# A hand-written order with two copies on another engine, some tasks in other places and one buffer in another slot

## The chip, the cores and the metric

The kernel runs on one core of a Trainium2 chip. The metric is the time of one execution on the device in microseconds (us), as the median of several runs. The kernel before takes 345.94 us in the median of three runs (345.81 to 346.79).

The engines of the core are TensorE (PE in the profile, PEld for its weight loads), VectorE (DVE), ScalarE (ACT), GpSimd (POOL) and SyncE (SP). SP and POOL do little but issue transfers (DMA) here. Every engine works through its own list of instructions in order; where one needs another's result, or a buffer that another still uses, it waits, and all that stands behind it in its list waits too.

## The reference

Two independent layers for a sequence of 2048 steps and 1024 channels; their outputs stand side by side.

```python
def _A_ref(q, k, v, shift_k, ssm_k, ssm_D):
    for t in range(ks):                      # ks = 4
        k_shift = k_shift + k_pad[:, t:t + S, :] * shift_k[:, ks - 1 - t][None, None, :]
    kv = k_shift * v
...
    y_f = kv_f * kf_f[None, :, :, :]         # Fourier transforms of kv and of ssm_k, length 2 S
    y = irfft2(y_f)[:, 0, :S, :]
    y = y + kv * ssm_D[None, None, :]
    return q * y

def _B_ref(x, Lambda_re, Lambda_im, B_re, B_im, C_re, C_im, log_dt, Dskip):
...
    Bu = jnp.einsum("bld,pd->blp", x + 0j, B_bar)
    for t in range(L):
        h = Lam_bar[None, :] * h + Bu[:, t, :]
        hs.append(h)
    y = 2.0 * jnp.einsum("blp,dp->bld", hseq, Cmat).real + x * Dskip[None, None, :]
    return y
...
return jnp.concatenate([a, b], axis=-1)
```

Layer A is a long convolution, done by Fourier transforms; layer B is a linear recurrence with complex coefficients.

## The kernel before

The whole program is one list of some 1,500 words, `ORDER`. A word names a task, its arguments and the buffers that it takes, such as `sh.20:p5p6`: task sh for group 20, in the PSUM banks 5 and 6. A loop at the end of `full_kernel` goes through the words and calls the task's function, so the words' order is the order of the instructions on every engine, and the letters behind the colon say which buffer is used: `p` one of 8 PSUM banks, `a` a place in an arena of 53 units in SBUF, `h` one of three state buffers, `w` one of three tables. A task whose buffer is still in use waits. Nothing else decides the schedule.

Layer B goes through 16 chunks i of 128 steps. `U.i.jp.jl` forms the inputs of the recurrence on PE (16 products of 128x128, line L464), `ue.i.jp` copies them from PSUM (L473). On DVE follow `r1.i` and `r2.i` (a rotation: product and sum, L487 and L498), two scans `sc.i` (L504), and `r3.i` and `r4.i`, which rotate back (L487 and L510). `yq.i.k` (L538) or `y.i.dh.part` (L520, L523) form the output on PE, `ye.i.dh` copies it from PSUM (L556), `ysp.i` writes it out from SP's queue (L564), `ysg` and `ysh` write halves (L560). `x.i` loads a chunk of the input, transposing it (L447). Ahead of the loop stand the tables of the rotation (`tabA1`, `tabA2`, `par_rest`) and the transposed weights: `bT.j.w` transposes on PE (L415), `bc.j.w` on ACT (L431) or `bcv.j.w` on DVE (L427, L429) copies.

Layer A does the transform in two stages with matrix products. The first (`am`, `ae`) goes through memory; the second works on 32 groups g, two to an index i = g // 2. `lh.i` and `lk.i` load the two operands (L677), `lw.i` the table (L672). `sh.g` and `sk.g` are products of 64x64 with the table (four each, L688), `she.g.l` (L697) and `ske.g.l` (L704) copy them from PSUM. `sw.i.q` (from POOL) and `swp.i.q` (from SP) copy one half of a buffer with its real and imaginary rows swapped (L708). `pr.i` multiplies the two spectra on DVE (L714). `sa.g` transforms back on PE (eight products, L726), `sae.g.dh` copies (L734), `vst.i` writes to memory (L737), `vl.n` loads back (L742), `a3.n.dh` is the last stage on PE (two products, L754), `a3e.n.dh` copies (L761), `qp.r` loads q (L747), `qm.r` multiplies with q on DVE (L763), and `osp` and `ost` write out.

A copy from PSUM is a task in two variants, made by one helper:

```python
def either(nm, f):
    E[nm] = lambda *a: f(nc.scalar.copy, *a)
    E[nm + "v"] = lambda *a: f(nc.vector.tensor_copy, *a)
```

So `ye.10.1` runs on ACT and `yev.10.1` on DVE.

Of the kernel before, what the change touches and what calls it, by code (L numbers as in the profile page):

```python
# [156 lines left out]
r3.11:a17 sh.30:p4p0 sh.31:p2p6 U.12.3.1:p3 she.20.0 she.31.0:a9 sw.10.1 U.12.3.0 lk.10:a45 U.12.0.0:p5 she.30.1
she.31.1 lk.12:a39 she.30.0 ue.12.3 lk.15:a43 swp.10.0 swp.15.0 U.12.0.1 sa.22:p4p3 r4.11 sae.22.0:a37 sa.23:p1p2
U.12.2.0:p6 sae.23.1 sw.15.1 U.12.2.1 uev.12.2 ue.12.0 sae.23.0 sk.20:p0p5 sae.22.1 ske.20.0:a28 sk.21:p7p2 skev.21.0
yq.11.0:p4p1 sk.30:p6p0 ske.20.1 ske.30.1:a18 yq.11.1 sk.31:p3p0 yq.11.2 lw.12:w1 vst.7 lk.14:a47 ske.30.0 ske.31.0  # L160
sh.25:p3p7 yq.11.3 skev.21.1 sh.24:p5p2 ske.31.1 pr.10 she.25.0:a24 sa.20:p0p3 she.25.1 sa.21:p7p6 she.24.1 yq.11.4
she.24.0 vst.11 pr.15 vst.9 sae.20.1:a29 sae.20.0 yq.11.5 r1.12:a2 sk.24:p3p2 sae.21.1 sa.31:p5p0 ysp.10 sae.31.1:a20
saev.31.0 lw.14:w0 yq.11.6 sa.30:p6p0 ske.24.0:a22 sae.30.0 skev.24.1 yq.11.7 saev.21.0 sk.25:p6p5 swp.12.0 sh.28:p7p2
sae.30.1 U.13.3.0:p0 yev.11.1:a28 ye.11.0 sk.29:p1p3 ske.25.1 cy.12:h1 shev.28.1:a16 ske.25.0 sk.28:p2p5 sh.29:p6p4
she.28.0 she.29.0 U.13.3.1 U.13.1.1:p7 r2.12 x.15:a0 ske.28.0:a5 ske.29.0 U.13.1.0 ske.28.1 U.13.2.1:p6 ue.13.3:a10
swp.12.1 lh.13:a13 sc.12.1 lw.13:w2 lk.13:a45 she.29.1 sh.26:p0p4 qp.0:a48 sw.14.1 ske.29.1 she.26.0:a41 sh.27:p5p3
she.27.0 U.13.2.0 pr.12 U.13.0.0:p2 she.27.1 she.26.1 ue.13.2 U.13.0.1 ue.13.1 sk.26:p3p1 swp.14.0 ske.26.0:a1
sk.27:p6p4 sa.25:p7p0 U.15.3.0:p5 ue.13.0 ske.27.1 sae.25.1:a38 sc.12.0 r3.12:a12 U.15.0.1:p2 U.15.3.1 pr.14 U.14.2.1:p3
U.15.0.0 sae.25.0 swp.13.1 ske.27.0 vst.15 ske.26.1 uev.15.3:a50 sw.13.0 sa.29:p7p6 sa.28:p0p1 ue.15.0 sa.24:p4p2 vst.6
ysp.11 sae.29.1:a34 U.15.1.0:p5 sae.24.0 r4.12 sae.24.1 qp.5:a6 vst.10 saev.29.0 sae.28.0 U.15.1.1 U.14.2.0 pr.13  # L170
sa.27:p6p4 ue.15.1 cy.13:h2 sae.28.1 sae.27.0:a8 yq.12.0:p0p7 r1.13:a12 sa.26:p1p2 yq.12.1 yq.12.2 saev.26.0 qp.6:a20
sae.27.1 yq.12.3 U.14.3.1:p5 U.14.1.0:p1 vst.12 sae.26.1 ue.14.2:a24 U.14.0.1:p3 U.14.3.0 vst.14 U.14.1.1 qp.1:a18
U.15.2.0:p4 vst.13 U.14.0.0 ue.14.3 yq.12.4 yq.12.5 ue.14.1 r2.13 sc.13.0 sc.13.1 vl.3:a38 r3.13:a12 r4.13 yq.13.0:p2p1
yq.13.1 yq.13.2 ue.14.0 yq.13.3 r1.14:a40 r2.14:h0 cy.14 vl.13:a44 yq.12.6 vl.1:a16 vl.9:a32 yq.12.7 a3.13.1:p5 sc.14.1
sc.14.0 r3.14:a24 a3e.13.1:a4 vl.2:a2 ye.12.0:a41 U.15.2.1 a3.13.0:p3 a3.1.0:p5 yq.13.4 vl.12:a46 yq.13.5 uev.15.2
# [667 lines left out]
```

## Time and profile before

| | |
|---|---|
| median of three runs | 345.94 us (345.81 to 346.79) |
| the profiled execution | 345.12 us |
| its span, first instruction to last | 343.4 us |
| PE busy | 331.0 us, 96% |
| DVE busy | 326.1 us, 95% |
| ACT busy | 273.0 us, 80% |
| POOL busy | 66.8 us, 19% |
| transfers of SP's queue, share of 16 DMA engines | 66.6% |
| transfers of POOL's queue, share of 16 DMA engines | 25.6% |

The span is the part of an execution in which the program's instructions run; the rest of the time lies around it. A row of the timeline has the start in us, the duration in us, the engine, the line, the operation, what it writes and reads, and how many neighbouring instructions of one form it merges; in brackets stands how long the engine sat idle before it, and what released it. A row of SP (SPq) is the issue of a transfer, not the transfer. Rows of PE merge groups of four or more products. A row of the busy time by stage gives for each engine the busy time and the number of instructions.

### The profile page before, as it was taken

Reading aid. Unit: us, or ns where it says so; the run is one execution under the profiler, and the core shown is the slowest. Engines: PE = TensorE matmul, PEld = TensorE weight load, DVE = VectorE, ACT = ScalarE, POOL = GpSimd, SP = SyncE. Lnnn points to the kernel's source line nnn. Section 1 sums busy time; section 2 is a strip of 40 time slices with the busy share of each in tenths; the row PEclk is TensorE's granted clock in tenths of the full one; section 3 lists DMA queues with packets and bytes.
Section 4 is the critical chain, followed back from the end, with each engine's and each line's share of the span. In section 5 each row is a group of like instructions: output and inputs, shape, how many; then the busy total and the mean of one; then the engine's idle time right before and its main releaser. Section 6 shows DMA issues by size and latency. Waiting matters only on the chain. (4 is left out here: it accounts for less than half of the span.)

```text
span 343.4 us, 11818 instructions
## 1 busy us (share of the span) xinstructions
PE 331.0 (96%) x5105; PEld 231.4 (67%) x5105; DVE 326.1 (95%) x262; ACT 273.0 (80%) x523; POOL 66.8 (19%) x108
## 2 busy tenths in 40 slices
...
GB/s 191 366 283 304 282 264 296 253 300 351 234 303 255 326 268 266 247 296 249 297 321 271 324 348 264 351 254 272 318 320 290 296 326 315 208 370 296 353 371 245
DMA packets 62944, 100.83 MB, mean 294 GB/s; under 512 B 29422, under 2 KB 31742, under 8 KB 62892
## 3 DMA queue, kind: packets, MB, share of 16 engines
q1 hardware_dynamic: 53452, 67.65, 66.6%
q0 software_dynamic: 9440, 32.42, 25.6%
q8 instruction: 40, 0.66, 0.8%
...
## 5 line engine op out<-in xcount | busy, mean ns | idle before, releaser
L464 PEld LDWEIGHTS <-BT 128*128 128x128 bf16 x2048 | 117.0, 98 | 13.8 <-issue 9.2
L464 PE MATMUL bank<-arena,BT 128*128 128x128 bf16 x2048 | 124.6, 220 | 0.3 <-ACT BT L431 0.3
L538 PE MATMUL bank<-CT,gslot 64*64 64x512 bf16 x1408 | 88.0, 378 | 0.0
L504 DVE TENSOR_TENSOR_SCAN gslot<-rtab,gslot 128x1040 bf16<-128x1040 f32 x32 | 72.9, 2310 | 0.8
L538 PEld LDWEIGHTS <-gslot 64*64 64x64 bf16 x1408 | 38.4, 107 | 30.2 <-issue 1.3
L473 ACT CAST arena<-bank 128x512 bf16<-128x512 f32 x61 | 37.1, 641 | 11.4 <-PE bank L464 10.5
L614 ACT CAST arena<-bank 128x512 bf16<-128x512 f32 x64 | 36.2, 646 | 7.8 <-PE bank L608 7.2
L520 PE MATMUL bank<-CT,gslot 128*128 128x512 bf16 x160 | 39.4, 379 | 0.1
L487 DVE TENSOR_TENSOR arena<-gslot,Z 128x4096 bf16<-128x4096 bf16 x16 | 36.6, 2288 | 0.5
L704 ACT CAST arena<-bank 128x512 bf16<-128x512 f32 x60 | 33.6, 612 | 4.3 <-PE bank L688 3.1
L714 DVE TENSOR_TENSOR arena<-arena 128x4096 bf16<-128x4096 bf16 x16 | 36.4, 2282 | 0.2
L487 DVE TENSOR_TENSOR arena<-arena,Z 128x4096 bf16<-128x4096 bf16 x16 | 36.5, 2282 | 0.0
L697 ACT CAST arena<-bank 128x512 bf16<-128x512 f32 x62 | 33.5, 618 | 3.7 <-PE bank L688 2.3
L734 ACT CAST arena<-bank 128x512 bf16<-128x512 f32 x60 | 32.9, 609 | 4.4 <-PE bank L726 4.3
L665 ACT CAST arena<-bank 128x512 bf16<-128x512 f32 x64 | 34.3, 631 | 1.9 <-PE bank L657 1.8
L588 DVE TENSOR_TENSOR arena<-arena 128x4096 bf16<-128x4096 bf16 (+3 forms) x16 | 29.9, 1881 | 0.0
L668 POOL DMA_DIRECT2D Ys_h<-arena x32 | 23.5, 737 | 28.5 <-ACT arena L665 26.0
L617 POOL DMA_DIRECT2D Ys_kv<-arena x16 | 11.1, 710 | 87.5 <-ACT arena L614 86.0
L761 ACT CAST arena<-bank 128x512 bf16<-128x512 f32 x26 | 13.7, 599 | 15.3 <-PE bank L754 15.1
L556 ACT CAST arena<-bank 128x512 bf16<-128x512 f32 x30 | 17.8, 602 | 9.7 <-PE bank L538 4.9
L520 PEld LDWEIGHTS <-gslot 128*128 128x128 bf16 x160 | 14.3, 98 | 16.5 <-issue 1.3
L688 PE MATMUL bank<-arena,wslot 64*64 64x512 bf16 x256 | 22.4, 382 | 0.8 <-DMA wslot<-a_c_W 0.8
...
## 6 DMA issues: line engine op xcount, KB each, us to landing
...
Ys_h<-arena POOLq DMA_DIRECT2D x32, 256.0 KB, 4.7
...
arena<-arena SPq DMA_DIRECT2D x17, 256.0 KB, 4.0
...
```

Source lines behind the costliest of these rows:

```text
L464: nc.tensor.matmul(pu[:, w, jl, :], BT[:, 2 * jp + jl, w, d, :], xT[:, d, :], start=(d == 0), stop=(d == ND - 1))
L473: cp(st["u", i][:, :, 2 * jp:2 * jp + 2, :], st.pop(("pu", i, jp)))
L487: nc.vector.tensor_mul(m, s_, win(Z))
L504: nc.vector.tensor_tensor_scan(gf, rtab[:].rearrange("p j t -> p (j t)"), gf, 0.0, ALU.mult, ALU.add)
L520: nc.tensor.matmul(py, h[:, w, j, 2:GW], CT[:, j, w, dh * 512:(dh + 1) * 512], start=(j == 0 and w == 0), stop=False)
L538: mm = nc.tensor.matmul(st["py", i, dh][cols, cs(r)], lhs(dh, rows, c), rhs(dh, rows), start=first, stop=last)
L614: cp(st["ysb", n2][:, p, dh * 512:(dh + 1) * 512], st.pop(("pa", n2, p, dh)))
L665: cp(o, st.pop(("pb", hf, s, e, r)).rearrange("p (n c t) -> p n c t", n=2, c=2))
L697: cp(st["hab", i][:, 0, a, l, :], st.pop(("ps", "h", g, l)))
L704: cp(st["x16", i][:, a, l, :], st.pop(("ps", "k", g, l)))
L714: nc.vector.tensor_mul(hab, st.pop(("x16", i)).rearrange("p a l d -> p (a l d)").unsqueeze(1).to_broadcast([P, 2, 2 * D]), hab)
L734: cp(st["vsb", i][:, a, dh * 512:(dh + 1) * 512], st.pop(("pv", g, dh)))
```

## The change

Only the list changes; the same tasks run with the same arguments. Three words change in themselves, and twelve words stand in other places:

- `yev.10.1` becomes `ye.10.1` and `uev.15.2` becomes `ue.15.2`: two copies from PSUM go from DVE to ACT.
- `lh.13` takes the arena's places from 37 on instead of 13.
- `tabA1`, `bT.6.0`, `bcv.6.0` and `tabA2` stand together behind `sin0`, some places sooner.
- `U.3.1.0` stands three tasks of PE sooner, and names the bank in place of `U.3.1.1`.
- `ye.9.1` and `ysp.9` stand later, `ysp.9` behind `lw.10`.
- `sae.19.0`, `sh.20` and `she.20.1` stand together ahead of `sh.21`.
- `swp.15.0` stands behind `lw.12`.
- `a3.14.0` stands ahead of `a3.10.0`, `a3.11.0` and `a3.15.0`.

```diff
-yq.10.5 yq.10.6 r1.11:a19 r2.11 sae.14.1 sae.18.1 yq.10.7 sc.11.1 sh.21:p1p3 U.12.1.1:p7 ye.10.0:a42 yev.10.1
-shev.21.0:a5 lw.15:w2 lh.12:a1 sae.19.0 sh.20:p5p6 she.20.1 she.21.1 U.12.1.0 sw.11.1 pr.11 ue.12.1:a22 sc.11.0
...
+yq.10.6 r1.11:a19 r2.11 sae.14.1 sae.18.1 yq.10.7 sae.19.0 sh.20:p5p6 she.20.1:a5 sc.11.1 sh.21:p1p3 U.12.1.1:p7
+ye.10.0:a42 ye.10.1 shev.21.0 lw.15:w2 lh.12:a1 she.21.1 U.12.1.0 sw.11.1 pr.11 ue.12.1:a22 sc.11.0 r3.11:a17 sh.30:p4p0
```

SP's list around x.12, the second transposing load below, with rows merged where they are alike. L677 to Ys_h are lh.14, lh.15 and lh.10, L564 is ysp.9, wslot0 is lw.10, wslot2 lw.15 and the lower wslot1 lw.12; the two of L708 are swp.10.0 and swp.15.0.

```order
 L672 DMA wslot1_93<-a_c_W3 128x640
-L677 DMA arena_95<-Ys_h_87 128x2x1024 x2
-L564 DMA out_0_dram<-arena_95 128x1024
-L677 DMA arena_95<-Ys_h_87 128x2x1024
+L677 DMA arena_95<-Ys_h_87 128x2x1024 x3
 L447 DMA_TRANSPOSE arena_95<-in_B_x_dram 128x8x128
 L672 DMA wslot0_92<-a_c_W3 128x640
+L564 DMA out_0_dram<-arena_95 128x1024
 L672 DMA wslot2_94<-a_c_W3 128x640
```

ysp.9 went from ahead of lh.10 to behind lw.10. Further down, swp.15.0 goes in the same way from ahead of lw.12 to behind it.

ACT's list at the same time of the program. Banks 5 and 6 are those of sa.19 and sh.20, banks 0 and 2 those of chunk 10's output, bank 3 is sh.21's and bank 7 U.12.1's.

```order
 L734 CAST arena_95<-bank1_97 128x512
+L734 CAST arena_95<-bank5_101 128x512
+L697 CAST arena_95<-bank6_102 128x512
 L556 CAST arena_95<-bank0_96 128x512
-L734 CAST arena_95<-bank5_101 128x512
-L697 CAST arena_95<-bank6_102 128x512
+L556 CAST arena_95<-bank2_98 128x512
 L697 CAST arena_95<-bank3_99 128x512
 L473 CAST arena_95<-bank7_103 128x2x256
```

sae.19.0 and she.20.1 went ahead of ye.10.0, and ye.10.1 came over from DVE.

DVE's list at the same place: the sum r2.11, the scan sc.11.1, the two copies and pr.11.

```order
 L498 TENSOR_TENSOR gslot0_89<-arena_95 128x16x128
 L504 SCALAR_TENSOR_TENSOR gslot0_89<-rtab_79,gslot0_89 128x1040
-L556 CAST arena_95<-bank2_98 128x512
 L697 CAST arena_95<-bank1_97 128x512
 L714 TENSOR_TENSOR arena_95<-arena_95 128x4096
```

The copy yev.10.1 is gone; shev.21.0 follows the scan. Further down, uev.15.2 is gone from between r3.14 and r4.14 in the same way.

More of the change, by code (lines that the diff above doesn't have):

```diff
@@ L89 @@
-kvc.4 hst.0.4.1 y.0.1.1 he.0.6.0.1 r4.1 y.0.1.2 hm.0.0.1:p0p5 hc.0.2:a20 hm.0.7.0:p4p7 he.0.7.0.1:a50 y.0.1.3 r1.2:a15
-hst.0.4.0 he.0.0.1.1:a48 hm.0.0.0:p2p3 hm.0.5.1:p7p5 y.1.1.0:p1 hst.0.6.0 he.0.7.0.0 kvm.6:a38 he.0.0.1.0 he.0.0.0.1
-y.1.1.1 he.0.5.1.0:a23 he.0.0.0.0 hm.0.5.0:p4p2 he.0.5.1.1 he.0.5.0.1 vp.3:a26 am.4.0:p0p7 ye.0.1 he.0.5.0.0
+bT.0.1:p2 sin0 tabA1:a46a49a42a44 bT.6.0:p5 bcv.6.0 tabA2 bc.0.0 kp.1:a0 wb.1:p6 wb.6:p7 bc.0.1 wb.5:p3 kp.0 bT.1.0:p1
+wbe.1 bl.5.1:a23 sin1 wbe.6 par_rest wbe.5 bl.1.1:a27 bT.2.0:p2 sin2 dd bT.5.0:p3 bl.4.0:a39 bT.4.1:p7 bl.2.1:a25
@@ new lines @@
+U.1.0.0:p4 bT.5.1:p6 bc.1.0 x.0:a38 bl.3.0:a48 eo kvm.3:a29 kp.-1 bT.1.1:p5 bT.4.0:p0 bcv.1.1 bcv.4.1 bc.5.1 kva.3
+U.1.0.1 ue.1.0:a34 bl.3.1:a19 bc.4.0 U.0.0.0:p5 U.0.0.1 bl.7.0:a41 bT.2.1:p4 bl.6.1:a12 U.0.2.0:p0 bT.3.1:p7 bc.5.0
+U.0.2.1 bT.7.0:p6 stt ue.0.0:a24 bl.7.1:a20 bc.2.0 bc.2.1 x.2:a52 bT.6.1:p2 bT.7.1:p3 cl.1.0:a15 kp.-2 bT.3.0:p4 bc.7.0
+kring bc.3.1 x.3:a21 bc.3.0 U.1.2.1:p5 bc.7.1 U.1.2.0 cl.1.1:a37 U.1.1.1:p1 bc.6.1 U.1.1.0 cl.3.1:a14 U.0.3.1:p4 ue.0.2
+ue.1.2 kvm.1:a16 z2 kvm.2:a42 U.0.3.0 rta kva.1 kva.2 z1 U.0.1.0:p7 kvb.1:a39 cT.1.0:p6 U.3.0.1:p3 ue.0.3 kvb.2:a12
@@ new lines @@
+U.0.1.1 ue.0.1 cc.1.0 cT.3.1:p0 vp.1:a27 kvm.0:a16 cl.0.1:a48 kvb.3:a26 kva.0 kvc.3 cc.3.1 ld_Q ue.1.1 vp.0:a40
+kvb.0:a36 U.3.0.0 cx.5.1 cl.2.0:a13 U.3.2.0:p5 am.3.1:p7p2 ae.3.1.1:a19 r1.0:a29 kvc.2 U.3.2.1 ae.3.0.1 cl.0.0:a47
+am.3.0:p6p4 cx.7.0 kvc.1 ae.3.1.0 ae.3.0.0 cT.1.1:p1 cl.2.1:a44 U.3.1.0:p2 cT.0.1:p0 cT.0.0:p7 U.3.1.1 cc.1.1 cx.6.0
+U.3.3.1:p4 cl.3.0:a42 ue.3.2:a46 kp.2 cT.2.1:p5 gz r2.0:h1 kvc.0 ue.3.0 sc.0.0 sc.0.1 am.2.1:p1p3 cc.0.0 U.1.3.0:p7
+cc.0.1 hl.0.1:a23 cT.3.0:p6 r3.0:a27 ue.3.1 U.3.3.0 ae.2.0.1:a40 U.1.3.1 cc.2.1 cc.3.0 U.2.0.1:p2 hl.1.0:a48 ae.2.1.1
@@ new lines @@
+am.0.0:p0p3 ue.3.3 ue.1.3 ae.0.0.0:a43 ae.0.1.0 am.0.1:p4p5 ae.0.1.1 r1.3:a15 U.2.0.0 ue.2.0:a36 am.1.1:p0p6 hl.0.0 r4.0
+U.2.2.0:p1 hl.1.1 ae.0.0.1 ast.0 am.1.0:p2p7 ae.1.0.1:a45 U.2.2.1 cx.6.1 r2.3:h2 ast.3 hT.0.1:p4 r1.1:a27 hT.0.6:p3
+ae.1.1.0 U.2.3.1:p7 kvm.4:a14 ae.1.1.1 ue.2.2 cx.4.1 ae.1.0.0 r2.1:h0 hd.0 am.2.0:p6p5 hc.0.1:a22 U.2.3.0 ae.2.1.0 ast.1
+cx.7.1 hd.1 ue.2.3 cT.2.0:p1 ae.2.0.0 hT.0.3:p2 cc.2.0 hc.0.6:a32 U.2.1.0:p7 U.2.1.1 hc.0.3:a13 hT.0.7:p0 hm.0.6.1:p4p1
+hT.0.4:p6 cx.4.0 cy.1 kva.4 y.0.0.0:p3 ue.2.1 ast.2 sc.1.1 hc.0.4:a28 sc.1.0 hc.0.7:a12 y.0.0.1 hm.0.4.0:p2p6 kvb.4:a31
@@ new lines @@
+he.0.6.1.0:a43 he.0.4.0.1:a29 he.0.4.0.0 he.0.6.1.1 hT.0.0:p5 cx.5.0 hT.0.5:p0 vp.2:a34 y.0.0.2 hT.0.2:p1 r3.1:a45
+hc.0.0:a19 hm.0.6.0:p6p2 he.0.6.0.0 hm.0.4.1:p5p4 he.0.4.1.1 he.0.4.1.0 y.0.0.3 hst.0.6.1 y.0.1.0:p6 kp.3 ye.0.0:a25
+hc.0.5:a14 kvc.4 hst.0.4.1 y.0.1.1 he.0.6.0.1 r4.1 y.0.1.2 hm.0.0.1:p0p5 hc.0.2:a20 hm.0.7.0:p4p7 he.0.7.0.1:a50 y.0.1.3
+r1.2:a15 hst.0.4.0 he.0.0.1.1:a48 hm.0.0.0:p2p3 hm.0.5.1:p7p5 y.1.1.0:p1 hst.0.6.0 he.0.7.0.0 kvm.6:a38 he.0.0.1.0
+he.0.0.0.1 y.1.1.1 he.0.5.1.0:a23 he.0.0.0.0 hm.0.5.0:p4p2 he.0.5.1.1 he.0.5.0.1 vp.3:a26 am.4.0:p0p7 ye.0.1 he.0.5.0.0
@@ L156 @@
-shev.21.0:a5 lw.15:w2 lh.12:a1 sae.19.0 sh.20:p5p6 she.20.1 she.21.1 U.12.1.0 sw.11.1 pr.11 ue.12.1:a22 sc.11.0
[L157 to L175, printed above, removed]
@@ L176 @@
-yq.13.6 yq.13.7 ye.12.1 a3e.13.0 a3e.1.0:a34 r4.14 r1.15:a22 cy.15:h1 a3.2.1:p4 a3.3.1:p7 vl.6:a8 vl.10:a28 ye.13.0:a11
+ske.19.0 ye.9.0:a3 ske.22.0:a15 sk.18:p7p3 ske.18.1 sc.10.1 r3.10:a46 r4.10 lh.10:a47 ye.9.1 ske.18.0 ske.22.1 pr.7
+yq.10.0:p0p2 yq.10.1 pr.9 sk.23:p3p4 yst.7 yq.10.2 ske.23.1 ske.23.0 sa.15:p5p1 yq.10.3 x.12:a52 sa.14:p7p3 lw.10:w0
+sae.15.1:a24 sae.15.0 ysp.9 sae.14.0 sa.18:p6p1 sa.19:p5p4 cy.11:h0 yq.10.4 ld_G sae.19.1:a49 sae.18.0 sw.11.0 yq.10.5
+yq.10.6 r1.11:a19 r2.11 sae.14.1 sae.18.1 yq.10.7 sae.19.0 sh.20:p5p6 she.20.1:a5 sc.11.1 sh.21:p1p3 U.12.1.1:p7
@@ new lines @@
+ye.10.0:a42 ye.10.1 shev.21.0 lw.15:w2 lh.12:a1 she.21.1 U.12.1.0 sw.11.1 pr.11 ue.12.1:a22 sc.11.0 r3.11:a17 sh.30:p4p0
+sh.31:p2p6 U.12.3.1:p3 she.20.0 she.31.0:a9 sw.10.1 U.12.3.0 lk.10:a45 U.12.0.0:p5 she.30.1 she.31.1 lk.12:a39 she.30.0
+ue.12.3 lk.15:a43 swp.10.0 U.12.0.1 sa.22:p4p3 r4.11 sae.22.0:a37 sa.23:p1p2 U.12.2.0:p6 sae.23.1 sw.15.1 U.12.2.1
+uev.12.2 ue.12.0 sae.23.0 sk.20:p0p5 sae.22.1 ske.20.0:a28 sk.21:p7p2 skev.21.0 yq.11.0:p4p1 sk.30:p6p0 ske.20.1
+ske.30.1:a18 yq.11.1 sk.31:p3p0 yq.11.2 lw.12:w1 swp.15.0 vst.7 lk.14:a47 ske.30.0 ske.31.0 sh.25:p3p7 yq.11.3 skev.21.1
@@ new lines @@
+sh.24:p5p2 ske.31.1 pr.10 she.25.0:a24 sa.20:p0p3 she.25.1 sa.21:p7p6 she.24.1 yq.11.4 she.24.0 vst.11 pr.15 vst.9
+sae.20.1:a29 sae.20.0 yq.11.5 r1.12:a2 sk.24:p3p2 sae.21.1 sa.31:p5p0 ysp.10 sae.31.1:a20 saev.31.0 lw.14:w0 yq.11.6
+sa.30:p6p0 ske.24.0:a22 sae.30.0 skev.24.1 yq.11.7 saev.21.0 sk.25:p6p5 swp.12.0 sh.28:p7p2 sae.30.1 U.13.3.0:p0
+yev.11.1:a28 ye.11.0 sk.29:p1p3 ske.25.1 cy.12:h1 shev.28.1:a16 ske.25.0 sk.28:p2p5 sh.29:p6p4 she.28.0 she.29.0
+U.13.3.1 U.13.1.1:p7 r2.12 x.15:a0 ske.28.0:a5 ske.29.0 U.13.1.0 ske.28.1 U.13.2.1:p6 ue.13.3:a10 swp.12.1 lh.13:a37
@@ new lines @@
+sc.12.1 lw.13:w2 lk.13:a45 she.29.1 sh.26:p0p4 qp.0:a48 sw.14.1 ske.29.1 she.26.0:a41 sh.27:p5p3 she.27.0 U.13.2.0 pr.12
+U.13.0.0:p2 she.27.1 she.26.1 ue.13.2 U.13.0.1 ue.13.1 sk.26:p3p1 swp.14.0 ske.26.0:a1 sk.27:p6p4 sa.25:p7p0 U.15.3.0:p5
+ue.13.0 ske.27.1 sae.25.1:a38 sc.12.0 r3.12:a12 U.15.0.1:p2 U.15.3.1 pr.14 U.14.2.1:p3 U.15.0.0 sae.25.0 swp.13.1
+ske.27.0 vst.15 ske.26.1 uev.15.3:a50 sw.13.0 sa.29:p7p6 sa.28:p0p1 ue.15.0 sa.24:p4p2 vst.6 ysp.11 sae.29.1:a34
+U.15.1.0:p5 sae.24.0 r4.12 sae.24.1 qp.5:a6 vst.10 saev.29.0 sae.28.0 U.15.1.1 U.14.2.0 pr.13 sa.27:p6p4 ue.15.1
```

32 lines of the change are left out of this document (8 added, 24 removed).

## The prediction

> **What bounds the kernel now.** I read the summary page first, then busy time by stage, then the chain that ended last, then the engines' timelines where the change lies. Names such as sh.20 are those of the order; a timeline row merges tasks of one line.
>
> ```profile
> span 343.4 us, 11818 instructions
> ...
> 20.00:236.00 216.00, 214.78 (x3455) 155.50 (x3456) 215.21 (x159) 193.43 (x365) 48.18 (x71) 1.00 0.95 288
> 236.00:288.00 52.00, 51.19 (x956) 36.62 (x960) 50.48 (x34) 42.20 (x85) 8.66 (x14) 1.00 0.94 313
> 288.00:328.40 40.40, 40.19 (x516) 23.02 (x508) 39.86 (x28) 16.72 (x34) 1.85 (x3) 1.00 0.89 305
> ...
> 327.25 1.15 DVE gslot L510
> ...
> 328.44 1.04 PE bank L520 x4
> ...
> 337.73 0.59 ACT arena L556
> ```
>
> The stage rows give PE, PEld, DVE, ACT and POOL in this order. PE and DVE are both full in the first three, so the kernel has two bounds at once. ACT has 9.8 us free in the second stage and 23.7 in the third. The chain ends with r4.15 on DVE (L510), which releases the last products on PE at 328.44; 9.3 us of PE work and the last output follow whatever happens before. So the question is how much earlier r4.15 ends, and whether PE is there in time. Between 20 and 236 us DVE is 0.8 us short of full; no edit takes work from it there. What can move the end lies behind 236 us.
>
> **The change part by part.** First the early moves: four tasks in the first 15 us, U.3.1.0 near 40 us.
>
> ```profile
> 14.23 0.68 DVE L429 COPY BT<-bank 128x1024 bf16<-128x1024 bf16 x1
> 14.83 2.28 DVE L588 TENSOR_TENSOR arena<-arena 128x4096 bf16<-128x4096 bf16 x1
> 17.23 1.29 DVE L427 TENSOR_SCALAR BT<-bank 128x1024 bf16<-128x1024 bf16 x2
> ```
>
> On DVE they permute the same instructions, with the copy of 0.68 us (bcv.6.0) some places sooner. The one gap in these rows is 0.12 us before 17.23 (14.83 + 2.28 = 17.11). I take 0, since the order of DVE's other work stays and covers the moved steps; the bounds are a gain of 0.12, all of that gap, and a loss of 0.68, if bcv.6.0, now ahead of the tables' second half, waited for its transposes by its own length. U.3.1.0 stands 16 products sooner on a PE that is full either way: 0.
>
> **ysp.9.** In SP's queue it goes behind lw.10; this term decides.
>
> ```profile
> 237.73 0.35 SPq L564 DMA_DIRECT2D out_dram<-arena  x1
> 238.76 1.84 SPq L447 DMA_TRANSPOSE arena<-in_B_x_dram  x1
> 240.88 1.17 SPq L672 DMA_DIRECT2D wslot<-a_c_W  x2
> ...
> 240.21 1.46 PE L726 MATMUL bank<-arena,wslot 64*64 64x512 bf16 x24
> ...
> 246.08 0.41 PE L688 MATMUL bank<-arena,wslot 64*64 64x512 bf16 x4 [0.81 <-DMA wslot<-a_c_W]
> 246.42 1.07 PE L464 MATMUL bank<-arena,BT 128*128 128x128 bf16 x16
> 247.42 0.41 PE L688 MATMUL bank<-arena,wslot 64*64 64x512 bf16 x4
> 247.76 1.07 PE L464 MATMUL bank<-arena,BT 128*128 128x128 bf16 x16
> 248.76 0.63 PE L688 MATMUL bank<-arena,wslot 64*64 64x512 bf16 x8
> 249.31 3.75 PE L464 MATMUL bank<-arena,BT 128*128 128x128 bf16 x64
> 252.99 1.06 PE L726 MATMUL bank<-arena,wslot 64*64 64x512 bf16 x16
> ...
> GB/s 344 295 213 328 377 311 311 361 377 148 164 221 205 336 213 197 295 311 385 393 352 279 344 336 401 410 394 309 209 114 47 31 15 94 290 373 384 272 389 414
> ...
> out_dram<-arena SPq DMA_DIRECT2D x1, 256.0 KB
> ```
>
> The one clear hole in PE's second stage is the 0.81 us before 246.08: sh.21 waits for the table lw.10, the first of the two at 240.88. lw.10 cannot be issued sooner: it waits for the table's last reader, sa.14, the first 8 of the 24 products at 240.21. But 256 KB of output (ysp.9, 237.73) stand ahead of it in the same queue, and the bandwidth slices (236 to 246 us) show the transfers at 336 to 410 GB/s just before they thin out. 256 KB at 390 GB/s are 0.66 us. With ysp.9 behind lw.10 I take that: PE goes on at 245.42. Bounds: 0, if lw.10 waits for something else, and 0.81, the whole hole.
>
> **sh.20** goes next to sh.21, ahead of U.12.1.1. Now PE runs four products, 16, four, 16: from 246.08 to 248.76, 2.68 us, with two changes of form. The pair sh.30 and sh.31 shows what two neighbours cost: 249.31 less 248.76, 0.55. A U followed by another form takes 1.00 (246.42 to 247.42); four in a row take 3.68 (249.31 to 252.99), so one followed by another U (3.68 - 1.00) / 3 = 0.89. The new order takes 0.55 + 0.89 + 1.00 = 2.44. PE gains 0.24; bounds 0 and 0.34, one whole sh (246.08 to 246.42). sh.20 needs the bank that sae.19.0 empties: ACT will do that ahead of ye.10.0, in the time in which it waits at present.
>
> **The two copies,** yev.10.1 and uev.15.2, go from DVE to ACT; with them stand DVE's waits.
>
> ```profile
> 244.09 2.33 DVE L504 TENSOR_TENSOR_SCAN gslot<-rtab,gslot 128x1040 bf16<-128x1040 f32 x1
> 246.33 0.66 DVE L556 CAST arena<-bank 128x512 bf16<-128x512 f32 x1
> 246.91 0.68 DVE L697 CAST arena<-bank 128x512 bf16<-128x512 f32 x1
> ...
> 256.05 0.69 DVE L473 CAST arena<-bank 128x512 bf16<-128x512 f32 x1 [0.44 <-PE bank L464]
> ...
> 287.56 0.69 DVE L734 CAST arena<-bank 128x512 bf16<-128x512 f32 x1 [0.43 <-PE bank L726]
> ...
> 293.99 2.29 DVE L487 TENSOR_TENSOR arena<-gslot,Z 128x4096 bf16<-128x4096 bf16 x1
> 296.32 1.23 DVE L510 TENSOR_TENSOR gslot<-arena 128x2048 bf16<-128x2048 bf16 x1
> ...
> 305.68 2.29 DVE L487 TENSOR_TENSOR arena<-gslot,Z 128x4096 bf16<-128x4096 bf16 x1
> 307.89 0.68 DVE L473 CAST arena<-bank 128x512 bf16<-128x512 f32 x1
> 308.49 1.21 DVE L510 TENSOR_TENSOR gslot<-arena 128x2048 bf16<-128x2048 bf16 x1
> ...
> 245.35 0.59 ACT L556 CAST arena<-bank 128x512 bf16<-128x512 f32 x1 [1.57 <-PE bank L538]
> ```
>
> Starts count, since neighbours overlap by some 0.09. Without yev.10.1 shev.21.0 starts at 246.33 instead of 246.91: 0.58. That alone would be lost, because DVE then waits longer at 256.05 for U.12.2.1 and at 287.56 for sa.26: both times PE sets the end of the wait. Up to 287.56 DVE therefore gains what PE gains, 0.66 + 0.24 = 0.90, as long as this is below 0.58 + 0.44 + 0.43 = 1.45. uev.15.2 lies behind the last such wait. It fills the place between r3.14 and r4.14, 308.49 - 305.68 = 2.81; the same pair with nothing between takes 296.32 - 293.99 = 2.33. So it brings 0.48, not its 0.60. DVE at r4.15: 0.90 + 0.48 = 1.38. ACT gets a new wait: she.20.1 stands ahead of ye.10.0 and waits for sh.20, which ends about 245.42 + 0.41 = 245.8. Behind it follow ye.10.0 and the copy that came over; at the full 0.59 each the three end by 247.6, and sh.30 and sh.31, which need the two banks, come at 245.42 + 2.44 = 247.9. ACT takes uev.15.2 in the third stage, where it has 23.7 us to spare.
>
> The Trainium skill, "VectorE: DVE Perf Modes", section "The DRAIN you can't avoid", says that the next instruction does not start until the pipe is empty. By it a copy that goes would give its whole length; for uev.15.2 that is 0.68 in place of 0.48, and the sum would be 0.90 + 0.68 = 1.58. The rows speak against it: the copy at 246.33 starts 0.09 before the scan ends.
>
> **The end:** is PE there in time, with a3.14.0 two places sooner?
>
> ```profile
> 327.30 0.53 PEld L754 LDWEIGHTS <-Gt 128*128 128x128 bf16 x3 [0.41 <-issue]
> 328.43 0.12 PEld L520 LDWEIGHTS <-gslot 128*128 128x128 bf16 x2 [0.61 <-DVE gslot L510]
> ...
> 331.90 3.50 DVE L763 TENSOR_TENSOR arena<-arena 128x2048 bf16<-128x2048 bf16 x3 [1.12 <-DMA arena<-in_A_q_dram]
> ```
>
> PE's gain at the end is its 0.90 and the slack that it has there: its loads stood idle 0.41 and 0.61 us. The first is a3.4.0, whose bank holds a3.14.0 until DVE has copied it, the second r4.15; both releases come sooner with DVE, and half of the 1.02 is what PE needs to follow by 0.48 more. I take all of it: 1.38, between 0.90 and 1.38. The other output's last products on DVE (three at 331.90, behind 1.12 us of waiting for a load) end at 335.40, 2.3 us before ACT's last copy at 337.73 begins; a3.14.0's earlier place frees that load's buffers, so I cost them at nothing.
>
> **swp.15.0 and lh.13** (behind lw.12, and in another buffer): 0 each. lh.13 no longer waits for the old buffer's reader, so it and lw.13 behind it are issued no later. swp.15.0 is rival D; a gain is excluded, since it is only put back. lw.15, which ysp.9's issue of 0.35 now precedes, is first read by sh.30 at 248.76, 6.7 us behind its issue.
>
> **Sum.** The profiled execution took 345.12 us, 1.72 more than its span. 345.12 - 1.38 = 343.74. It lies 0.82 below the median of the runs, 345.94, so against that median: 344.56, which I call 344.6. With the two PE terms at their bounds the gain goes from 0.48 to 0.81 + 0.34 + 0.48 = 1.63; a loss in the early moves can take up to 0.68 of it.
>
> **Rivals.** B: lw.10 lands no sooner. The bandwidth slices fall to 15 GB/s just before it lands: that is the transposing load at 238.76, and if its end is set by itself, ysp.9 was not in the way. PE gains 0.24 and the whole is 0.24 + 0.48 = 0.72: 345.2. For it speaks the hole in the slices; against it, that the queue was full up to the hole, so that the hole too would come sooner. The Trainium skill, "DMA: Bandwidth & Descriptors", section "Queues, rings and completion order", says that completion is not first in, first out, and a later transfer may finish its write before an earlier one. By that rule lw.10 need not have waited for ysp.9, which is this rival.
>
> C: the DVE time is lost again in a new wait. DVE and PE end within tenths of each other in every stage, so a bank or a load that I did not follow can take the 1.38 back to between 0 and 0.3: some 345.8. Against it: ACT, which takes the two copies, is the engine with room.
>
> D: slower, by swp.15.0. The rows are lw.12's issue, DVE's pr.10 and pr.15, and how long all transfers of the swapping line took to land.
>
> ```profile
> 254.10 0.34 SPq L672 DMA_DIRECT2D wslot<-a_c_W  x1
> ...
> 258.03 4.49 DVE L714 TENSOR_TENSOR arena<-arena 128x4096 bf16<-128x4096 bf16 x2
> ...
> DMA to landing us min/median/max: 3.2/4.2/7.4
> ```
>
> swp.15.0 hands a swapped half to the product pr.15 and stands ahead of lw.12 now. Behind lw.12, which waits for sa.23 (254.10 now, 0.90 sooner then), it goes 0.4 later, at 253.6. pr.15, the second of the two at 258.03, starts half way through them, at about 260.3 now and at 259.4 then. Landing of such a transfer (last row: shortest, median, longest) takes 4.2 in the median: 257.8, in time. It decides from a landing of 5.8 us. At the longest, 7.4, pr.15 waits until 261.0, 1.6 late: 1.38 - 1.6, so 0.2 slower, 346.1; at 8.2 it would be 1.04 slower, 347.0.
>
> That the change does something else than it says is hardly open: the order rows show both copies gone from DVE. Only ye.9.1 moves on no engine.
>
> **How the numbers follow.** Forecast (gain 0.95 to 1.63): 0.52. B: 0.25. C: 0.14. D: 0.09. A measurement tells about 0.3%, 1.04 us, from no change. Faster by more: nearly all of the forecast and, with the scatter, a fifth of B, 0.54. Within: the rest of both, C and a third of D, 0.40. Slower by more: the rest of D, 0.06. The forecast's own range is 344.3 to 345.0. With B, C and the scatter of the runs (345.81 to 346.79, 0.5 either way) the range is 343.9 to 346.0.
>
> **What would show it.** PE's wait for the table before sh.20 down to about 0.15 us, its first L688 product near 245.4 and U.12.1.0 ended 0.90 sooner; DVE's wait at 256 shorter, not gone; DVE's copy of sa.26 near 286.7; r4.14 2.33 us behind r3.14; r4.15 ending near 327.0. The prediction is wrong if the table's wait is unchanged, if pr.15 waits for a transfer, or if a new wait on ACT or a load stands in DVE's rows between 246 and 328 us.

## The result, and the profile after

The changed kernel takes 343.96 us in the median of 21 runs (343.27 to 345.81); the kernel before took 346.07 in 21 runs beside it (345.00 to 348.87). The ratio is 0.9947, with a 95% interval of 0.9934 to 0.9961: 1.83 us faster (1.35 to 2.28). The ratio is estimated from all the runs; the two medians alone lie 2.11 us apart. The forecast was 1.38. Its profiled execution took 343.27 us, the fastest of the 21; that of the kernel before, at 345.12, also lies near the lower end of its runs.

The page's first line and the busy time by stage of the changed kernel (columns PE, PEld, DVE, ACT, POOL):

```profile
span 341.4 us, 11817 instructions
...
20.00:236.00 216.00, 214.82 (x3454) 156.24 (x3455) 214.82 (x159) 192.68 (x364) 47.72 (x70) 1.00 0.96 288
236.00:288.00 52.00, 52.00 (x976) 36.96 (x972) 50.98 (x35) 43.91 (x88) 9.12 (x14) 1.00 0.96 322
288.00:328.40 40.40, 40.35 (x505) 23.15 (x498) 39.64 (x27) 17.54 (x36) 1.85 (x3) 1.00 0.89 311
```

PE's 0.8 us of idle time in the second stage are gone, and ACT is busy for 1.7 us more there. The timeline of the changed kernel at the places of the prediction, first PE, then DVE:

```profile
245.66 0.60 PE L688 MATMUL bank<-arena,wslot 64*64 64x512 bf16 x8
246.20 1.96 PE L464 MATMUL bank<-arena,BT 128*128 128x128 bf16 x32
248.09 0.63 PE L688 MATMUL bank<-arena,wslot 64*64 64x512 bf16 x8
...
149.46 2.29 DVE L487 TENSOR_TENSOR arena<-arena,Z 128x4096 bf16<-128x4096 bf16 x1 [0.48 <-DMA Ys_kv<-arena]
...
255.49 0.68 DVE L473 CAST arena<-bank 128x512 bf16<-128x512 f32 x1
...
286.97 0.69 DVE L734 CAST arena<-bank 128x512 bf16<-128x512 f32 x1 [0.44 <-PE bank L726]
...
305.09 2.29 DVE L487 TENSOR_TENSOR arena<-gslot,Z 128x4096 bf16<-128x4096 bf16 x1
307.42 1.22 DVE L510 TENSOR_TENSOR gslot<-arena 128x2048 bf16<-128x2048 bf16 x1
```

sh.20 and sh.21 are now one row of eight products, and no bracket stands behind it: the table lay ready. But everything stood 0.57 us later here than before (r4.10, below, starts at 235.25 and not at 234.68), for DVE had waited for a store at 149.46, which it did not in the profile of before. r4.14 follows r3.14 by 2.33 us (307.42 - 305.09), as forecast. Now the end, in the timelines of the kernel before and of the changed kernel:

```profile
234.68 1.22 DVE L510 TENSOR_TENSOR gslot<-arena 128x2048 bf16<-128x2048 bf16 x1
...
325.41 0.83 SPq L747 DMA_DIRECT2D arena<-in_A_q_dram  x2
...
333.42 0.72 POOL L764 DMA_DIRECT2D out_dram<-arena  x1 [2.35 <-DVE arena L763]
...
338.34 0.34 SPq L560 DMA_DIRECT2D out_dram<-arena  x1
```

```profile
235.25 1.22 DVE L510 TENSOR_TENSOR gslot<-arena 128x2048 bf16<-128x2048 bf16 x1
...
323.96 0.83 SPq L747 DMA_DIRECT2D arena<-in_A_q_dram  x2
...
330.21 1.23 DVE L763 TENSOR_TENSOR arena<-arena 128x2048 bf16<-128x2048 bf16 x1 [0.28 <-DMA arena<-in_A_q_dram]
...
331.73 0.71 POOL L764 DMA_DIRECT2D out_dram<-arena  x1 [1.45 <-DVE arena L763]
...
336.81 0.59 ACT L556 CAST arena<-bank 128x512 bf16<-128x512 f32 x1 [3.09 <-PE bank L523]
337.42 0.34 SPq L560 DMA_DIRECT2D out_dram<-arena  x1
```

ACT's last copy starts 0.92 us sooner (336.81 against 337.73), but the span is 2.0 shorter. The other 1.08 lie behind that copy: 343.4 - 338.32 = 5.08 us before, 341.4 - 337.40 = 4.00 now, in which only the last output is issued and lands. The forecast had no term there. Divided at three places (r4.10's end, PE's wait for the table, the end of ACT's last copy), the 2.0 us are: 0.57 lost ahead of r4.10's end (235.90 before, 236.47 now), 0.81 won in the wait, 0.68 in the rest up to the last copy (the forecast's 0.24 and 0.48 are 0.72), 1.08 behind it.

### The profile page after: what moved, and what is told of

Same layout as the page of the kernel before. It is cut to its first block, busy times and chain, and to the rows that moved or that the text cites. A ratio compares the mean times of both kernels' runs of the same rounds, so it can differ in the third digit from the quotient of the medians.

```text
span 341.4 us, 11817 instructions
## 1 busy us (share of the span) xinstructions
PE 330.6 (97%) x5105; PEld 231.6 (68%) x5105; DVE 325.1 (95%) x260; ACT 274.1 (80%) x525; POOL 66.8 (20%) x108
```

## The experiments

Theories: **F**, the forecast's own terms; **R**, the edits costed at nothing bring what is missing; **T**, which says how, the tail: a3.14.0's place makes layer A's last loads and outputs sooner, and the last output lands sooner behind its issue; **E**, the early moves, swp.15.0 or lh.13 bring it; **B**, the transposing load x.12 and not ysp.9 holds the table. All gains below come from ratios, times 346 us.

**ysp.9 alone.** The kernel before with

```diff
-sc.10.1 ye.9.1 ysp.9 r3.10:a46 r4.10 lh.10:a47 ske.18.0
+sc.10.1 r3.10:a46 r4.10 lh.10:a47 ye.9.1 ske.18.0
...
-sae.15.0 sae.14.0
+sae.15.0 ysp.9 sae.14.0
```

> Before, with ysp.9 (and ye.9.1, which moves on no engine) put where the changed kernel has it; nothing else. Theory F (the forecast's own terms): the table lw.10 lands about 0.66 us sooner after the transposing load x.12 begins, PE's wait ahead of sh.21 shrinks by about 0.66 and the end comes 0.66 us sooner (0.2%). Theory B (ysp.9 was not in the way): x.12 and lw.10 land as long after x.12's issue as before (6.8 and 7.3 us), gain 0. Theory R (the edits costed at nothing bring what the forecast lacked): as F, 0.66 at the most.

345.86 us, ratio 0.9986 (0.9967 to 1.0004), a gain of 0.5 us at an interval from -0.1 to 1.1. PE waited 1.62 us for the table, not less than the 0.81 of before but more. As a size it decides nothing; the wait of this one execution speaks against F.

**The three tasks alone**, and **the two copies alone**:

```diff
-yq.10.7 sc.11.1
+yq.10.7 sae.19.0 sh.20:p5p6 she.20.1:a5 sc.11.1
...
-shev.21.0:a5 lw.15:w2 lh.12:a1 sae.19.0 sh.20:p5p6 she.20.1 she.21.1
+shev.21.0 lw.15:w2 lh.12:a1 she.21.1
```

> Before, with sae.19.0, sh.20 and she.20.1 moved ahead of sh.21 as in the changed kernel; yev.10.1 stays on DVE, ysp.9 where it was. Theory F: PE still waits for the table until about 0.8 us after yq.10.7, but from its first product with the table to the end of U.12.1.0 it takes 2.44 instead of 2.68 us: 0.24 us sooner at the end (0.07%). Rival: DVE, which keeps its copy yev.10.1, sets the pace behind it, and nothing is left: 0.

```diff
-ye.10.0:a42 yev.10.1
+ye.10.0:a42 ye.10.1
...
-yq.13.5 uev.15.2 yq.13.6
+yq.13.5 ue.15.2 yq.13.6
```

> Before, with yev.10.1 and uev.15.2 given to ACT as in the changed kernel; nothing else. Theory F: the first copy's 0.58 us are lost to DVE's waits at U.12.2.1 and sa.26, which grow by as much in sum; the second brings 0.48, so the end comes 0.48 us sooner (0.14%), r4.14 follows r3.14 by 2.33 instead of 2.81. Rival: PE is held by DVE somewhere between 246 and 288 us and gains from the first copy too: up to 1.06 us (0.3%).

Ratios 1.0002 (0.9977 to 1.0027) and 0.9995 (0.9975 to 1.0014): too small for these measurements of the time. Their profiles show them; those are read in the table below. The timeline of DVE with the copies alone, and what followed r4.14 in the kernel before:

```profile
306.22 2.29 DVE L487 TENSOR_TENSOR arena<-gslot,Z 128x4096 bf16<-128x4096 bf16 x1
308.55 1.23 DVE L510 TENSOR_TENSOR gslot<-arena 128x2048 bf16<-128x2048 bf16 x1
309.88 2.29 DVE L487 TENSOR_TENSOR arena<-arena,Z 128x4096 bf16<-128x4096 bf16 x1
312.27 1.22 DVE L498 TENSOR_TENSOR gslot<-arena 128x2048 bf16<-128x2048 bf16 x1
```

```profile
309.74 2.29 DVE L487 TENSOR_TENSOR arena<-arena,Z 128x4096 bf16<-128x4096 bf16 x1
312.06 1.23 DVE L498 TENSOR_TENSOR gslot<-arena 128x2048 bf16<-128x2048 bf16 x1
```

r4.14 follows r3.14 by 2.33 instead of 2.81: 0.48, as forecast. But the next two starts stand 1.33 and 2.39 apart instead of 1.25 and 2.32 (308.49 to 309.74 to 312.06), so 0.15 of it goes at once.

**What the forecast cost at nothing**, alone:

```diff
-bT.0.1:p2 sin0 bc.0.0
+bT.0.1:p2 sin0 tabA1:a46a49a42a44 bT.6.0:p5 bcv.6.0 tabA2 bc.0.0
...
-kp.1:a0 wb.1:p6 tabA1:a46a49a42a44 wb.6:p7
+kp.1:a0 wb.1:p6 wb.6:p7
...
-bl.1.1:a27 tabA2 bT.2.0:p2 sin2 bT.6.0:p5 dd
+bl.1.1:a27 bT.2.0:p2 sin2 dd
...
-bl.3.0:a48 bcv.6.0 eo
+bl.3.0:a48 eo
...
-cl.2.1:a44 cT.0.1:p0 cT.0.0:p7 U.3.1.1:p2
+cl.2.1:a44 U.3.1.0:p2 cT.0.1:p0 cT.0.0:p7 U.3.1.1
...
-cT.2.1:p5 U.3.1.0 gz
+cT.2.1:p5 gz
...
-swp.10.0 swp.15.0
+swp.10.0
...
-lw.12:w1
+lw.12:w1 swp.15.0
...
-lh.13:a13
+lh.13:a37
...
-a3e.5.0 a3.10.0:p5
+a3e.5.0 a3.14.0:p7 a3.10.0:p5
...
-qm.4 a3.14.0:p7
+qm.4
```

> Before, with only the edits that the forecast cost at nothing: the early moves (tabA1, bT.6.0, bcv.6.0, tabA2, U.3.1.0), swp.15.0 behind lw.12, lh.13 in another buffer, a3.14.0 two places sooner. Theory F: 0 (bounds of the early moves +0.12 and -0.68 us). Theory R: these bring what the forecast lacked, 1.83 - 1.38 = 0.45 us (0.13%), most likely at the end, where the last load qp.7 and the outputs behind it go sooner with a3.14.0, and the stretch from ACT's last copy to the end of the span is shorter than before (5.1 us there).

344.45 us, ratio 0.9941 (0.9922 to 0.9960): 2.0 us (1.4 to 2.7), as much as the whole change, and 4.1 us behind ACT's last copy. So the gain sits here, which F excludes. **Which of them** the next three kernels ask: a3.14.0 alone, the change without it, and another way to the same end; the fourth takes ysp.9 out of the change.

```diff
-a3e.5.0 a3.10.0:p5
+a3e.5.0 a3.14.0:p7 a3.10.0:p5
...
-qm.4 a3.14.0:p7
+qm.4
```

> Before, with only a3.14.0 moved two places ahead. Theory T (tail): a3.14.0 is the last reader of the buffer that the load qp.3 takes, and qp.7 stands behind qp.3 in SP's queue; with it sooner, both are issued about 1.4 us sooner, qm.7 no longer waits 1.1 us for its load, layer A's last outputs leave DVE sooner and are out of the last output's way: from ACT's last copy to the end of the span 4.0 to 4.2 us instead of the 5.1 to 6.1 of before, y_only, s_only and c_only, and a gain of 1.0 to 2.0 us (0.3 to 0.6%), most of what rest_only gained (2.0). Theory F: 0. Theory E (the gain of rest_only comes from the early moves, swp.15.0 or lh.13): 0 here.

345.08 us, ratio 0.9967 (0.9943 to 0.9991): 1.1 us (0.3 to 2.0), which F's 0 is outside of. The changed kernel with this edit undone:

```diff
-a3e.5.0 a3.14.0:p7 a3.10.0:p5
+a3e.5.0 a3.10.0:p5
...
-qm.4 a3.15.0:p0
+qm.4 a3.14.0:p7 a3.15.0:p0
```

> The changed kernel with a3.14.0 back in its old place. Theory T: the stretch behind ACT's last copy is 5.1 to 6.1 us again and most of the gain is gone: 0.2 to 0.9 us (0.05 to 0.25%) are left. Theory F: PE's gain at the end falls back from 1.38 towards 0.90 at worst, so 0.9 to 1.4 are left of it, 1.4 to 1.8 of the measured 1.83. Theory E: as the changed kernel, 1.8 us (0.5%).

345.76 us, ratio 0.9973 (0.9952 to 0.9994): 0.9 us are left (0.2 to 1.7), half of the gain; by itself this does not exclude F's 1.4. The other way, in the kernel before, touches no engine but SP:

```diff
-qp.3:a24 qp.7:a32
+qp.7:a32 qp.3:a24
```

> Before, with the load qp.7 ahead of qp.3 in SP's queue and nothing else: a3.14.0 stays where it was. qp.7's buffer is free early, qp.3's only behind a3.14.0. If theory T has the mechanism right (qm.7's load was late, and layer A's outputs crowd the last one), this does the same without touching PE's order: qm.7 starts right behind a3ev.7.0, the stretch behind ACT's last copy is 4.0 to 4.5 us, gain 1.0 to 1.8 us. If the place of a3.14.0 on PE and ACT itself matters (its bank, a3e.4.0's order), nothing is gained: 0 to 0.3.

345.46 us, ratio 0.9960 (0.9939 to 0.9981): 1.4 us (0.7 to 2.1), by the order of two loads alone. The ends of a3.14.0 alone and of the swapped loads, in their timelines:

```profile
324.78 0.83 SPq L747 DMA_DIRECT2D arena<-in_A_q_dram  x2
...
331.76 1.23 DVE L763 TENSOR_TENSOR arena<-arena 128x2048 bf16<-128x2048 bf16 x1 [0.73 <-DMA arena<-in_A_q_dram]
333.19 2.36 DVE L763 TENSOR_TENSOR arena<-arena 128x2048 bf16<-128x2048 bf16 x2 [0.21 <-ACT arena L761]
```

```profile
332.48 1.22 DVE L763 TENSOR_TENSOR arena<-arena 128x2048 bf16<-128x2048 bf16 x1
334.72 2.36 DVE L763 TENSOR_TENSOR arena<-arena 128x2048 bf16<-128x2048 bf16 x2 [1.03 <-ACT arena L761]
```

With the loads swapped qm.7 (332.48) has no bracket any more: its load is in time. The two products behind it then wait for a copy of ACT, so that they gain less; the output of qm.7's rows leaves sooner all the same. The gain is what T expected, with PE's list untouched, so a3.14.0's place on PE is not needed for it: the order of the loads is enough. Two readings fall short of T. The stretch behind ACT's last copy is 4.8 us in this profile and not 4.0 to 4.5, and with a3.14.0 alone qm.7 still waits 0.73 for its load, so that qm.7's wait is only a part of it; where the rest shows stands under the first point further down.

The changed kernel with ysp.9 and ye.9.1 back:

```diff
-sc.10.1 r3.10:a46 r4.10 lh.10:a47 ye.9.1 ske.18.0
+sc.10.1 ye.9.1 ysp.9 r3.10:a46 r4.10 lh.10:a47 ske.18.0
...
-sae.15.0 ysp.9 sae.14.0
+sae.15.0 sae.14.0
```

> The changed kernel with ysp.9 back ahead of lh.10 (and ye.9.1 back). Theory F: 0.66 us of the gain go, 1.2 of 1.83 are left. Rival (the transposing load x.12 sets the table's landing, and its own duration swings by more than ysp.9's 0.66): 0 to 0.3 go; x.12 lands 6.6 to 6.9 us behind its issue and lw.10 0.47 behind it, as in the four kernels in which ysp.9 stood ahead.

344.55 us, ratio 0.9934 (0.9911 to 0.9957): 2.3 us (1.5 to 3.1), no less than with ysp.9 moved; F's 1.2 lies outside. **The early moves alone**, that is the first six pieces of the long diff above, with the kernel before as the base:

> Before, with only the early moves (tabA1, bT.6.0, bcv.6.0, tabA2 behind sin0; U.3.1.0 three tasks sooner). Theory F: 0 (bounds +0.12 and -0.68 us); DVE's copy bcv.1.1 waits for the loads of the start by 0 to 1.2 us from run to run, with or without the moves. Theory E: what rest_only gained beyond a3_only (2.0 against 1.1 by the ratios) is theirs: 0.5 to 0.9 us (0.15 to 0.25%).

345.88 us, ratio 0.9992 (0.9969 to 1.0015). E gets no support. What moves at the start is the wait of bcv.1.1, with these moves and without them; DVE's rows in the profiles of ysp.9 alone and of the change without ysp.9:

```profile
17.77 1.29 DVE L427 TENSOR_SCALAR BT<-bank 128x1024 bf16<-128x1024 bf16 x2 [0.66 <-PE bank L415]
```

```profile
18.34 0.69 DVE L427 TENSOR_SCALAR BT<-bank 128x1024 bf16<-128x1024 bf16 x1 [1.22 <-PE bank L415]
```

DVE is nearly full from there on, and such a wait is carried along, not always whole: against the kernel before, these copies start 0.54 and 1.11 us later, and r4.10 ends 0.34 and 1.16 later. It is a part of the scatter of the kernels here.

**The transposing load sooner** in the changed kernel, to take PE's wait away, and the same with the loads swapped as above:

```diff
-lh.15:a43 yq.9.5
+yq.9.5
...
-yq.9.6 yq.9.7
+yq.9.6 yq.9.7 x.12:a52 lh.15:a43
...
-yq.10.3 x.12:a52 sa.14:p7p3
+yq.10.3 sa.14:p7p3
```

> The changed kernel with the transposing load x.12 (and lh.15 behind it) put right behind yq.9.7, the last reader of its buffer: in SP's queue it goes ahead of lh.15 and lh.10 instead of behind them, some 3 us sooner. If x.12's end sets when the table lw.10 lands (so far 0.45 to 0.62 us behind x.12 in all ten profiles), lw.10 now lands 3 to 4 us behind its own issue, by 245, PE does not wait for the table (0 to 1.6 us in the profiles so far) and the kernel gains 0.2 to 0.7 us over the changed kernel: 2.0 to 2.5 us over before (0.6 to 0.7%). If the table lands late for another reason (the two loads lh.15 and lh.10, 1 MB ahead of it), the wait stays and the gain is that of the changed kernel, 1.8 (0.53%).

> As x12_early, with qp.7 ahead of qp.3 as well. Theory T: qm.7's load is in time with a3.14.0's new place already to within 0.3 to 0.7 us, and qm.3 then waits for ACT's copy a3e.7.1 anyway; the stretch behind ACT's last copy shortens by 0 to 0.4 us against x12_early (4.0 to 4.5 us before that), so 0 to 0.4 us more gain.

Ratios 0.9981 (0.9952 to 1.0010) and 0.9952 (0.9924 to 0.9979): no better than the changed kernel. PE waits for the table for 2.13 and 2.18 us; only with the swapped loads, 2.25, was it longer. Its row with x.12 sooner, and the bandwidth in 40 slices from 236 to 246 us:

```profile
247.01 0.86 PE L688 MATMUL bank<-arena,wslot 64*64 64x512 bf16 x8 [2.13 <-DMA wslot<-a_c_W]
...
GB/s 229 295 312 372 311 165 195 240 201 68 26 105 17 101 66 44 199 78 65 294 82 43 105 379 352 197 393 393 385 393 385 451 369 330 366 362 346 383 433 378
```

The hole in the bandwidth came along: it begins at 238.25 now and ends near 241.75. Behind it lh.15 and lh.10, 1 MB, go through at 390 GB/s, and then the table. So the hole belongs to x.12, and the table waits in the queue for x.12 and for what stands between them. The expectation's first case failed. Of the second the wait came true, but it grew, and the gain is 0.7 us (-0.3 to 1.7) and not 1.8. Nor did the swapped loads shorten the stretch behind ACT's last copy here (4.28 against 4.22).

**The forecast's own edits together**, without those costed at nothing (the first three diffs above):

> Before, with just the edits that the forecast gave a price: ysp.9, the three tasks ahead of sh.21, the two copies; without the early moves, swp.15.0, lh.13 and a3.14.0. Theory F: 1.38 us (0.4%). Theory T: the pair sh.20, sh.21 brings its 0.24 and uev.15.2 its 0.48, as their rows show, ysp.9 something between -0.4 and 0.66 by the swing of x.12, and the stretch behind ACT's last copy stays at 5.1 to 6.1 us: 0.3 to 1.4 us, most likely 0.7 (0.2%). Without a3.14.0's new place qm.7 waits again for its load or an output buffer, by over 0.9 us.

346.37 us, ratio 1.0007 (0.9989 to 1.0026): 0.2 us slower, from 0.9 slower to 0.4 faster. F's 1.38 is outside, and of T's 0.3 to 1.4 only 0.3 to 0.4 is inside. The bandwidth from 236 to 246 us and PE's row here, and the bandwidth of the changed kernel:

```profile
246.92 0.63 PE L688 MATMUL bank<-arena,wslot 64*64 64x512 bf16 x8 [1.48 <-DMA wslot<-a_c_W]
...
GB/s 344 279 295 279 360 361 279 262 377 279 205 279 197 270 238 279 344 361 377 328 352 410 363 416 256 192 88 52 28 17 38 258 53 0 5 8 9 10 331 399
```

```profile
GB/s 377 344 377 295 246 279 426 311 328 344 393 189 205 262 369 320 336 328 287 344 393 418 352 346 373 288 172 70 35 17 9 118 291 362 358 331 418 377 379 424
```

Both have ysp.9 behind the table. In the changed kernel the hole lasts two us, from 242.25 to 244.25; here it breaks in two and lasts 3.5, from 242.0 to 245.5. That swing is larger than the 0.66 us that ysp.9 was to bring.

**All profiles in one table.** One execution of each kernel: PE's wait for the table; the time from r4.10's end to the end of ACT's last copy (in the kernel before 234.68 + 1.22 to 337.73 + 0.59, with hundredths from the unrounded records); the same less the wait; and from there to the end of the span as printed, to a tenth, so that the last column is good to 0.05.

| kernel | wait | r4.10 to last copy | less the wait | behind the copy |
|---|---|---|---|---|
| before | 0.81 | 102.41 | 101.60 | 5.09 |
| ysp.9 alone | 1.62 | 103.21 | 101.59 | 5.45 |
| early moves alone | 1.54 | 103.14 | 101.60 | 5.40 |
| the three tasks alone | 0.97 | 102.34 | 101.37 | 6.12 |
| the two copies alone | 1.02 | 102.29 | 101.27 | 5.69 |
| forecast's own edits | 1.48 | 102.57 | 101.09 | 5.95 |
| change without a3.14.0 | 0.74 | 101.79 | 101.05 | 6.09 |
| what was costed at nothing | 1.28 | 102.88 | 101.60 | 4.08 |
| a3.14.0 alone | 1.06 | 102.67 | 101.61 | 4.44 |
| qp.7 ahead of qp.3 | 2.25 | 103.92 | 101.67 | 4.81 |
| change without ysp.9 | 0.67 | 101.71 | 101.04 | 4.53 |
| the change | 0 | 100.92 | 100.92 | 4.01 |
| x.12 sooner | 2.13 | 104.76 | 102.63 | 4.22 |
| x.12 sooner, loads swapped | 2.18 | 103.31 | 101.13 | 4.28 |

Three things stand in it. The wait for the table goes into the end one to one: less the wait, six kernels with neither the three tasks nor the copies agree on 101.59 to 101.67. The three tasks take 0.23 off that, the copies 0.33, both together 0.5 to 0.7. The exception is x.12 sooner. There two U tasks behind the wait took 3.32 us, and 1.96 in the changed kernel, and the third figure from the end of the second row, a stage row, says why: the granted clock of PE, 0.50.

```profile
247.80 3.32 PE L464 MATMUL bank<-arena,BT 128*128 128x128 bf16 x32
...
247.30:250.60 3.30, 3.30 (x35) 2.81 (x28) 2.63 (x2) 2.05 (x4) 0.00 (x0) 0.50 0.99 364
```

Behind its wait PE ran at half its clock for 3.4 us. Behind the other two waits of over 2 us it did not. And the last column falls in two groups: 5.1 to 6.1 where a3.14.0 has its old place, 5.68 in the mean of seven, and 4.0 to 4.5 where it has the new one, 4.26 in the mean of six, a difference of 1.42; the swapped loads lie between.

## Why the prediction was right, and where it was not

The sign was right and the time came out inside the range, but by luck. 343.96 us lies 0.06 above the lower end of the range (343.9 to 346.0) and below the forecast's own 344.3 to 345.0. The edits that had a price bring, by themselves, nothing that can be told from zero (-0.2 us, -0.9 to 0.4), and those costed at nothing bring 2.0: the sum was put together from the wrong terms.

1. **The end: the step that failed.** It said that layer A's last products end 2.3 us before ACT's last copy begins and "I cost them at nothing". a3.14.0's new place measured 1.1 us by itself (0.3 to 2.0) and 1.42 by the table. DVE's work there was indeed off the path; its transfers were not. a3.14.0 is the last reader of the buffer that qp.3 loads into, and qp.7 stands behind qp.3. a3.14.0 ends sooner, the two loads are issued 1.45 us sooner (325.41 to 323.96), qm.7 waits 0.28 instead of 1.12, and the output that POOL issues behind it goes at 331.73 instead of 333.42, 1.69 sooner; 0.92 of these leads is what everything gained here, ACT's last copy too. The transfer engines are full nearly up to the end (98% busy before in the window further down), so that all of this stands ahead of the last output. From the last output's issue on, the packets show what still had to move, in the kernel before and in the changed one:

```profile
DMA packets 352, 0.69 MB, mean 135 GB/s; under 512 B 44, under 2 KB 222, under 8 KB 352
```

```profile
DMA packets 262, 0.53 MB, mean 132 GB/s; under 512 B 33, under 2 KB 166, under 8 KB 262
```

0.16 MB less, some 0.4 of the 1.08 us at 390 GB/s. What the place of a3.14.0 does shows before that, in the four us from 12 to 8 us ahead of the end of ACT's last copy; in order the kernel before, a3.14.0 alone and the swapped loads:

```profile
DMA packets 385, 1.36 MB, mean 339 GB/s; under 512 B 41, under 2 KB 41, under 8 KB 385
```

```profile
DMA packets 505, 1.67 MB, mean 417 GB/s; under 512 B 54, under 2 KB 54, under 8 KB 505
```

```profile
DMA packets 503, 1.65 MB, mean 414 GB/s; under 512 B 49, under 2 KB 49, under 8 KB 503
```

The seven kernels with a3.14.0 in its old place move 288 to 374 GB/s there, the six with the new one 368 to 417, though the engines count as 98 to 103% busy in all of them. The means, 327 and 403, are 0.3 MB apart, an estimated 0.8 of the 1.42 us. In all fourteen profiles the span ends 2.2 us behind the last packet; what differs is when the last packet ends: 2.8 to 3.9 us behind ACT's last copy with the old place, 1.8 to 2.4 with the new, 2.6 with the loads swapped. That the place of a3.14.0 makes the 1.42 is shown by the table; why equally busy engines move less in the old order is open.

2. **ysp.9: 0.66 forecast, nothing seen in the time.** One comparison gives 0.5 us for it (alone), one 0.5 against it (the change is 2.3 us faster than before without it, 1.8 with it), each well inside its interval. The four profiles with it have waits of 0, 0.74, 1.48 and 1.62 us, the eight without it, x.12 in its old place, 0.67 to 2.25. Rival B was nearer: the transposing load sets when the table lands, and its own swing covers the term. That x.12 is the holder is shown by moving it. The price itself has a basis in the packets: with ysp.9 behind the table x.12's first packet moves 5.5 to 5.8 us behind the end of r4.10, with ysp.9 ahead 6.5 to 6.8, a full us later. But from there to its last packet x.12 takes 2.4 to 4.1 us in the four and 2.3 to 3.7 in the eight, so that what reaches PE on average is not settled. PE's wait of 0 in the changed kernel, where 0.15 was forecast, is one draw from this; the same place of ysp.9 gave 0.74 without a3.14.0.

3. **The pair of sh: 0.24 forecast, 0.23 measured** by the table (101.60 to 101.37).

4. **uev.15.2: 0.48 forecast**, found at r4.14 to the hundredth, 0.33 left at ACT's last copy, since the two starts behind it moved apart by 0.15. yev.10.1 brought nothing of its own, as forecast: with the copies alone the table shows 0.33 in all, less than the 0.48 of uev.15.2.

5. **PE at the end** follows: y.15.1.0's products start 0.05 behind r4.15 in both profiles, and ACT's last copy gains the same 0.92 as r4.15. DVE's wait at 256, which was to be shorter, is gone (no bracket at 255.49). The early moves, swp.15.0 and lh.13 show nothing: 0.3 us for the early moves with an interval from -0.5 to 1.1, and pr.15 waits for no transfer in the profile, so rival D did not come. swp.15.0 and lh.13 by themselves were not tried. U.3.1.0 passes more of PE's list than was said: not three tasks or 16 products but five tasks, two of them U tasks of 16 products each; its term stays unseen.

Worked out from the table, the change is 1.42 + 0.55 = 1.97 us and what ysp.9 adds or takes; the measured 1.83 has that in its interval. Without the tail the forecast's parts come to 0.55, and the kernel that has only them is measured at -0.2 (-0.9 to 0.4). 0.55 lies outside that, and no run shows what takes it away; in its one profile PE waits 1.48 for the table, 0.67 more than before.

No version beat the changed kernel beyond its interval; without ysp.9 (0.9934), or with only the edits costed at nothing (0.9941), it is as fast.
